# A written-out instruction order with a new price list: TensorE's changes of tile form counted one by one, paces and ranks set anew

## The chip, the cores and the metric

The kernel runs on one core of a Trainium2 chip. The metric is the device time of one execution in microseconds (us). Five engines work side by side, each through its own queue in a fixed order: TensorE (PE, with its weight loads shown apart as PEld), VectorE (DVE), ScalarE (ACT), GpSimd (POOL) and SyncE (SP). SP does no arithmetic here; it issues most of the DMAs. An instruction that waits holds up everything behind it in its own queue.

## The reference

Two stages follow each other. First comes attention with a hash mask, for 4 batches, 8 heads, 768 positions and head size 64:

```
q_bits = (q @ proj > 0); k_bits = (k @ proj > 0)        # 6 bits each
mask   = bucket(q_bits)[:, None] == bucket(k_bits)[None, :]
scores = where(mask, q @ k.T / 8, -1e9)
attn   = exp(scores - rowmax) / (sum + 1e-9)
x      = attn @ v                                        # heads joined: 768 x 512 a batch
```

Then comes a gated block for each batch, whose second matrix product mixes positions:

```
h = relu(x @ w_in)                       # 512 -> 1024, split into u and v
v_n = (v - mean) / sqrt(var + 1e-6)
v_s = w_spatial @ v_n + b_spatial        # 768 x 768 times 768 x 512
out = (u * v_s) @ w_out                  # 512 -> 512
```

## The kernel before

**Precision.** Operands of TensorE are float16, and each float32 operand is split into a high and a low half; a product is then three matmuls (high by high, high by low, low by high). Where an operand is turned to halves, ACT writes the high one and DVE or POOL subtracts it to get the low one. That is why "splits" and "rests" fill the vector engines.

**Attention.** Two heads make a pair; there are 16 pairs, four to a batch. A pair has six score steps, one for each block of 128 rows, so 96 steps in all; step S3.1 below is block 1 of pair 3 (pairs count from 0). A step (function `scores`, line 501) is 16 matmuls: three split products and one that adds the mask, which is made from the hash signs in the tile hk. They write two PSUM tiles sp, one for each head, and there is only one such pair of tiles to hand out, so **the next step cannot start before both heads' scores have been read**. For most heads (`by_queries`) DVE reads them with a running row maximum (ex<-sp, L525), ACT or POOL makes the bias (L532, L530), ACT takes the exponential (L535) and the high half (L539), DVE or POOL subtracts to get the low half (the "rest", pp<-ex,pp, L543), and SP issues a transposing DMA (pt<-pp, L547). A few steps later TensorE multiplies the result by v (pv, L653). Four heads, in pairs 1 to 4, go another way (`by_keys`): scores are computed turned, so no transpose is needed, but the row maxima must be known beforehand. For them TensorE computes half-price scores first (mx, `row_max`), DVE reduces them (L600), and at a pair's end a small vector of maxima is turned by TensorE (tp), copied by DVE (mt, L624) and sent by a DMA from SP into a row of the mask tile (hk<-mt, L627). The first score step of the next pair needs that DMA in its last four matmuls.

**The hash.** Before a pair begins, TensorE multiplies q and k by proj (hp, L371), DVE makes signs and scales them (sg, L378 and L382), and POOL issues eight or twelve small DMAs that put them into hk (hk<-sg, L393). The pair's q and k are split by ACT (L412) and DVE (hl, L416).

**The gated block.** As soon as a batch's four pairs are done, its work is queued in groups of matmuls (line 750): vps (x by the v half of w_in), ups (the u half), sps (the spatial product) and ops (the output). They fill TensorE between the score steps of the next batch. Before batch 0 is through, that is up to pair 4, no such filler exists. The last batch's block comes behind all scores. The weights come in 36 pieces; a piece is fetched by SP (raw or raws, L293), of which there are four places, and for the double-precision weights taken apart by DVE (w, L313 to L318) before it is halved (wi, ws, wo, L323 on ACT and L328 on DVE).

**What sets the order.** The kernel first lists every operation as an `Op`, with its engines, a length in the planner's own units, what it needs and a rank. The function `timetable` then plays a list scheduler over the five engines: whichever engine can start soonest takes the ready operation with the lowest key. Score steps have keys of their own and may not start before a pace (`begin`, which grows by one of the constants T_ from step to step). Where two engines can do an operation ("VG" for DVE or POOL, "AG" for ACT or POOL), the engine that comes free first takes it. LATE is an allowance added before a TensorE operation, other than a score step, that waits for another engine. W_EVERY spaces the weights' fetches in the plan. LATER shifts ranks by the operation's function name. Where the plan shows TensorE idle for over GAP it fills the hole with small matmuls that are thrown away (`warm`, L217). The operations are then written down in order of planned start. **Nothing of the plan's clock reaches the chip**: only the order on each engine, the choice of engine, and the number of warm matmuls do.

## Time and profile before

| | |
|---|---|
| median of 3 runs | 660.48 us (660.45 to 661.58) |
| the profiled execution's own time | 655.07 us |
| its span, first to last instruction | 653.3 us |
| PE busy | 615.5 us (94%) |
| DVE busy | 471.1 us (72%) |
| ACT busy | 473.7 us (73%) |
| POOL busy | 321.8 us (49%) |
| warm matmuls | 444 |
| rests (L543) on DVE and on POOL | 82 and 86 |

The profiled execution took 5.4 us less than the median of the runs, and 1.8 us of it lie outside the span. Busy time of an engine is the union of its instructions; a matmul's row is longer than the time to the next matmul, since they overlap. Views that group instructions give the count, the busy time, the mean length in ns, and then the idle time just before them with what ended it. A view by stages gives busy time of each engine in a stretch of the span.

### The profile page before, as it was taken

What the parts mean: (1) busy time and instruction counts of PE and PEld (TensorE: products, weight loads), DVE (VectorE), ACT (ScalarE), POOL (GpSimd) and SP (SyncE); (2) the same over time, 40 slices, a digit from 0 to 9 for tenths busy, and PEclk for the clock granted to TensorE, in tenths of its full rate; (3) what the DMA queues carried; (4) which work ended last, traced back from release to release, by engine and by line L of the source; (5) the groups of instructions that cost most, each with busy time, mean ns of one, the idle gap of its engine ahead of it and who ended that gap; (6) DMA issues with size and microseconds to landing.
All of it is one profiled execution on the core that took longest, in us unless ns stands there. A gap on an engine that the chain in (4) does not pass through costs nothing.

```text
span 653.3 us, 17683 instructions
## 1 busy us (share of the span) xinstructions
PE 615.5 (94%) x7076; PEld 374.4 (57%) x7076; DVE 471.1 (72%) x986; ACT 473.7 (73%) x800; POOL 321.8 (49%) x397
## 2 busy tenths in 40 slices
PE   5789999899999999899999999998999999999997
PEld 3466767577555656455555556564555665556553
DVE  6899999898788766758879677765667587365250
ACT  3868776868898977887879887876889967463121
POOL 4565451534686859494638559376749412000000
PEclk9999999999999999999999999999999999999999
DMA  5899988997899999999998999997997989210102
GB/s 186 197 190 227 199 163 174 222 214 145 178 209 188 169 219 198 204 209 198 212 207 147 201 225 148 227 213 138 210 214 130 153 150 158 50 49 0 49 1 96
DMA packets 311682, 108.94 MB, mean 167 GB/s; under 512 B 298144, under 2 KB 301744, under 8 KB 311600
## 3 DMA queue, kind: packets, MB, share of 16 engines
q1 hardware_dynamic: 306256, 106.26, 84.4%
q0 software_dynamic: 5248, 1.52, 1.2%
q8 instruction: 55, 0.90, 0.6%
q14 instruction: 27, 0.22, 0.1%
q10 hardware_dynamic: 96, 0.04, 0.0%
HBM read 27.94 MB, written 6.29 MB: 52 GB/s over the span
## 4 chain that ended last, share of the span: by engine, by line
PE 51%; DVE 15%; DMA 11%; ACT 9%; issue 7%; POOL 5%; SPq 1%; DVEq 0%; POOLq 0%; ACTq 0%
PE sps L750 12%; PE sp L496 9%; PE ops L750 9%; PE pv L653 8%; DMA pt<-pp 6%; PE ups L750 5%; DVE ex L525 4%; PE vps L750 3%; ACT pp L539 3%; ACT ex L535 2%; POOL pp L543 2%; DVE pp L543 2%; PE vpp L750 2%; DMA hk<-sg 2%; DVE mx L600 1%
## 5 line engine op out<-in xcount | busy, mean ns | idle before, releaser
L525 DVE TENSOR_SCALAR_CACHE_REDUCE ex<-sp 128x768 f32<-128x768 f32 x168 | 155.6, 951 | 55.1 <-PE sp L496 53.0
L543 POOL TENSOR_TENSOR pp<-ex,pp 128x768 f16<-128x768 f32 x86 | 140.9, 1646 | 74.2 <-ACT pp L539 53.0
L535 ACT ACTIVATE ex<-ex,nb 128x768 f32<-128x768 f32 x168 | 155.3, 932 | 10.5 <-POOL nb L530 7.3
L539 ACT CAST pp<-ex 128x768 f16<-128x768 f32 x168 | 137.3, 826 | 4.9 <-DMA pt<-pp 3.6
L653 PEld LDWEIGHTS <-pt 128*128 128x128 f16 x3024 | 107.4, 97 | 37.3 <-DMA pt<-pp 13.3
L653 PE MATMUL pv<-vp,pt 128*128 128x65 f16 x3024 | 118.6, 193 | 7.9 <-DMA pt<-pp 7.7
L496 PE MATMUL sp<-hl 64*128 64x384 f16 x1080 | 107.4, 324 | 5.0 <-DVE ex L525 4.7
L393 POOL DMA_DIRECT2D hk<-sg x156 | 79.8, 518 | 50.8 <-issue 15.9
L543 DVE TENSOR_TENSOR pp<-ex,pp 128x768 f16<-128x768 f32 x82 | 79.7, 980 | 34.2 <-ACT pp L539 33.9
L750 PE MATMUL sps<-ws,vn 128*128 128x384 f16 x576 | 100.8, 326 | 0.1
L496 PEld LDWEIGHTS <-hl 64*128 64x128 f16 x1116 | 51.1, 94 | 56.8 <-issue 27.5
L750 PEld LDWEIGHTS <-vn 128*128 128x128 f16 x576 | 53.7, 98 | 33.5 <-issue 0.9
L750 PE MATMUL ops<-wo,g 128*128 128x512 f16 x288 | 66.1, 379 | 1.0 <-DVE sg L378 1.0
L532 ACT ACTIVATE nb<-mr 128x1 f32<-128x1 f32 x123 | 24.1, 197 | 55.9 <-DVE ex L525 55.6
L750 PE MATMUL ups<-xt,wi 128*128 128x384 f16 x348 | 62.8, 326 | 1.2 <-ACT u L919 1.2
L750 PE MATMUL vps<-wi,xt 128*128 128x512 f16 x234 | 56.9, 379 | 1.7 <-DVE sg L378 0.9
L750 PEld LDWEIGHTS <-wi 128*128 128x128 f16 x384 | 35.1, 98 | 24.1 <-issue 3.7
L750 PEld LDWEIGHTS <-g 128*128 128x128 f16 x288 | 26.7, 98 | 31.7 <-issue 1.6
L750 PEld LDWEIGHTS <-xt 128*128 128x128 f16 x288 | 25.5, 97 | 29.5 <-issue 5.4
L496 PE MATMUL sp<-hk 12*128 12x384 f16 (+2 forms) x360 | 37.1, 329 | 4.5 <-DMA hk<-mt 3.5
L940 DVE SCALAR_TENSOR_TENSOR sy<-sps,bt 128x384 f32<-128x384 f32 x32 | 17.8, 555 | 31.0 <-PE sps L750 31.0
L948 ACT CAST g<-sy 128x384 f16<-128x384 f32 x32 | 16.2, 506 | 32.3 <-DVE sy L952 28.8
(112 smaller groups left out, 786.7 us busy)
## 6 DMA issues: line engine op xcount, KB each, us to landing
qk<-kq SPq DMA_DIRECT2D x16, 768.0 KB
out<-o SPq DMA_DIRECT2D x24, 256.0 KB
v<-v SPq DMA_DIRECT2D x12, 384.0 KB
pt<-pp SPq DMA_TRANSPOSE x168
hk<-sg POOLq DMA_DIRECT2D x156, 9.0 KB, 4.0
raw<-w_in SPq DMA_DIRECT2D x8, 256.0 KB
raws<-w_in SPq DMA_DIRECT2D x8, 256.0 KB
vf<-v SPq DMA_DIRECT2D x4, 384.0 KB
```

Of the source, the lines that this page charges most:

```text
L393: eng.dma_start(out=hkt(p)[D * e + at:D * e + at + 2 * NB, 1 - j // 2, (j % 2) * HS:(j % 2 + 1) * HS], in_=sg[1][32 * j + 16 * e:32 * j + ...
L496: nc.tensor.matmul(ps[e][:, c - halves[0]], lhsT=src[r, l, rows], rhs=src[r, m, cs], start=(a == 0), stop=(a == len(passes) - 1))
L525: nc.vector.tensor_scalar(ex, st["sc", p, i][e], -float(2 ** 28), None, op0=ALU.max, op1=ALU.max, accum_out=st["mx", n][:, i:i + 1])
L532: nc.scalar.activation(nb, mx, AF.Copy, scale=-ISQ)
L535: nc.scalar.activation(st["e32", n, i], st["e32", n, i], AF.Exp, bias=st["nb", n][:, i:i + 1], scale=ISQ)
L539: nc.scalar.copy(st["pp", n, i][:, 0], st["e32", n, i])
L543: eng.tensor_tensor(out=st["pp", n, i][:, 1], in0=st.pop(("e32", n, i)), in1=st["pp", n, i][:, 0], op=ALU.subtract)
L600: nc.vector.reduce_max(st["mx", 2 * p + e][:, i, c:c + 1], ps[e], axis=AX.XY)
L653: nc.tensor.matmul(o, lhsT=l, rhs=m, start=(i == 0 and k == 0), stop=(i == NT - 1 and k == len(todo_) - 1))
L750: nc.tensor.matmul(c[0], lhsT=l(), rhs=r(), start=(j == 0), stop=(j == len(products) - 1))
L940: nc.vector.scalar_tensor_tensor(out=y[0], in0=c[0], scalar=1.0 / (SN * SW), in1=bt[:, hs], op0=ALU.mult, op1=ALU.add)
L948: nc.scalar.copy(gt[h][0][:, d], y[0])
```

## The change

The planner now keeps the tile form that TensorE was last used in (128 rows, 64 for scores, 1 for the hash product) and adds FORM = 0.1 to an operation of another form. In exchange the lengths of the score step, the hash product and the pv product are set lower. The ranks (LATER), the pace, START, LATE and W_EVERY get new values. No operation of the kernel is added or removed.

```diff
+    FORM = 0.1
     X = 0.14
-    LATER = {'relu': 0.1, 'first': -0.5, 'bias': -0.3, 'bits': 0.1, 'stats': 0.3, 'half': -0.4, 'copy': 0.6, 'scale': 0.3, 'newton': -0.4, 'low': 0.6, 'exp': -0.1, 'factor': -0.3, 'turn': -0.6, 'rest': -0.1}
+    LATER = {'relu': -0.2, 'first': -0.8, 'bias': -0.4, 'bits': -0.5, 'stats': -0.3, 'half': -1.0, 'copy': 0.5, 'scale': 0.6, 'newton': -0.7, 'low': 0.6, 'exp': -0.1, 'factor': -0.4, 'turn': -0.6, 'rest': -0.1, 'move': -0.2, 'root': 0.3, 'lambda': 0.1}
...
+        form = [128]
...
             gap = t - free[e]
+            if e == "P" and o.form != form[0]:
+                form[0], o.d = o.form, o.d + FORM
...
-        t = op("P", 0.8, go, at["qk", p], *after, on=[qk], rank=(urgent(p), 3), need=("m", 1))
+        t = op("P", 0.65, go, at["qk", p], *after, on=[qk], rank=(urgent(p), 3), need=("m", 1), form=1)
...
-        t = op("P", 1.32 if four(p) else 1.42, go, *at["hl", p], *at["hk", p], on=[sc, held["hl", p], held["hk", p]], rank=(g, 0))
+        t = op("P", 1.21 if four(p) else 1.27, go, *at["hl", p], *at["hk", p], on=[sc, held["hl", p], held["hk", p]], rank=(g, 0), form=64)
...
-        at["pv", n] = op("P", 1.46 if n in WIDE else 0.57, go, at["pt", n, i], at["v", p] if n in WIDE else at["vp", p],
+        at["pv", n] = op("P", 1.46 if n in WIDE else 0.56, go, at["pt", n, i], at["v", p] if n in WIDE else at["vp", p],
...
-    T_FIRST, T_KEYS, T_QUERIES, T_THIRD, T_LAST = 5.0, 5.4, 5.55, 5.75, 5.95
-    START = 6.5
+    T_FIRST, T_KEYS, T_QUERIES, T_THIRD, T_LAST = 5.1, 5.2, 5.75, 5.55, 5.85
+    START = 8.5
...
-    LATE, LATE_D = 0.3, 2.25
+    LATE, LATE_D = 0.1, 2.25
...
-    W_FROM, W_EVERY = 21.0, 2.1
+    W_FROM, W_EVERY = 21.0, 1.6
```

The order of the whole program is new from the first warm matmuls on; three places show the kind of thing that moved. (Line numbers of the changed kernel are five higher.)

**First place: DVE at the turn from pair 2 to pair 3.** ex5_5 is the read of step S2.5, ex7_0 that of S3.0, ex7_1 that of S3.1; sg0_4, hl4 and sg1_4 are the hash signs and the split for pair 4; ws, wi and w are weights. Before, from the last rest of pair 2 on:

```order
L543 TENSOR_TENSOR pp5_5_1873<-ex5_5_1825,pp5_5_1873 128x768
L378 TENSOR_SCALAR sg0_4_1892<-hp4_1876,hc_73 128x384
L416 SCALAR_TENSOR_TENSOR hl4_1883<-qk4_1289,hl4_1883 128x768 x2
L382 TENSOR_SCALAR sg1_4_1969<-sg0_4_1892,hc_73 128x384
L328 SCALAR_TENSOR_TENSOR ws1_80<-raw16_1818,ws0_79 128x384
L328 SCALAR_TENSOR_TENSOR ws1_80<-raw17_1827,ws0_79 128x384
L328 SCALAR_TENSOR_TENSOR wi1_102<-w15_1823,wi0_101 128x256
L328 SCALAR_TENSOR_TENSOR ws1_80<-raws_299,ws0_79 128x384
L525 TENSOR_SCALAR ex7_0_1986,mr7_1984<-sp3_0_1_1853 128x768
```

Now:

```order
L548 TENSOR_TENSOR pp5_5_1840<-ex5_5_1808,pp5_5_1840 128x768
L323 SCALAR_TENSOR_TENSOR w14_1801<-raws_294,w14_1801 128x256
L333 SCALAR_TENSOR_TENSOR wi1_102<-w13_1716,wi0_101 128x256
L530 TENSOR_SCALAR ex7_0_1897,mr7_1895<-sp3_0_1_1864 128x768
L383 TENSOR_SCALAR sg0_4_1919<-hp4_1887,hc_73 128x384
L421 SCALAR_TENSOR_TENSOR hl4_1893<-qk4_1317,hl4_1893 128x768 x2
L387 TENSOR_SCALAR sg1_4_1951<-sg0_4_1919,hc_73 128x384
L318 TENSOR_SCALAR w15_1947<-w15_1947 128x256
L530 TENSOR_SCALAR ex7_1_1975,mr7_1895<-sp3_1_1_1929 128x768
```

Four weight pieces, the hash signs and the split stood between the rest and the read of S3.0; now two other weight pieces do, and the signs and the split stand behind that read.

**Second place: SP's queue at the end of pair 3.** mt8 is the vector of maxima that step S4.0 needs, pt7_4 the transpose of step S3.4. Before:

```order
L293 DMA raws_299<-w_out 128x256
L547 DMA_TRANSPOSE pt7_4_2349<-pp7_4_2305 128x12x128
L627 DMA hk1_82<-mt8_2347 1x6x128
L547 DMA_TRANSPOSE pt7_5_2455<-pp7_5_2446 128x12x128
L293 DMA raws_299<-w_out 128x256
```

Now:

```order
L552 DMA_TRANSPOSE pt7_4_2306<-pp7_4_2245 128x12x128
L298 DMA raws_294<-w_sp 128x384
L298 DMA raw25_2349<-w_sp 128x384
L298 DMA raws_294<-w_sp 128x384
L632 DMA hk1_82<-mt8_2364 1x6x128
L552 DMA_TRANSPOSE pt7_5_2402<-pp7_5_2371 128x12x128
```

The transpose that was directly ahead of mt8 now has three weight fetches between it and mt8.

**Third place: DVE inside pair 5**, between the two reads of step S5.3 (ex10_3 and ex11_3). Before, two rows stood between them:

```order
L525 TENSOR_SCALAR ex10_3_3202,mr10_2955<-sp5_3_0_3167 128x768
L839 BN_STATS bs0_1_3210<-vr0_1_3200 128x6
L840 BN_AGGR mv0_0_3090<-bs0_1_3210 128x2
L525 TENSOR_SCALAR ex11_3_3253,mr11_2962<-sp5_3_1_3168 128x768
```

Now nine:

```order
L530 TENSOR_SCALAR ex10_3_3220,mr10_2912<-sp5_3_0_3129 128x768
L866 TENSOR_SCALAR ve0_0_3227<-mv0_0_2896 128x3
L421 SCALAR_TENSOR_TENSOR hl6_2909<-qk6_2760,hl6_2909 128x768
L876 TENSOR_TENSOR ve0_0_3227<-ve0_0_3227,rs0_0_3249 128x3
L877 SCALAR_TENSOR_TENSOR ve0_0_3227<-ve0_0_3227,rs0_0_3249 128x3
L878 SCALAR_TENSOR_TENSOR rs0_0_3249<-ve0_0_3227,rs0_0_3249 128x3
L879 SCALAR_TENSOR_TENSOR ve0_0_3227<-mv0_0_2896,rs0_0_3249 128x3
L421 SCALAR_TENSOR_TENSOR hl6_2909<-qk6_2760,hl6_2909 128x768
L844 BN_STATS bs0_4_3290<-vr0_4_3264 128x6
L845 BN_AGGR mv0_3_3210<-bs0_4_3290 128x2
L530 TENSOR_SCALAR ex11_3_3300,mr11_2940<-sp5_3_1_3130 128x768
```

The normalization of batch 0 and both splits for pair 6 have moved between the two reads. Counted over the program, DVE has 91 rests now and POOL 77 (82 and 86 before); the warm matmuls are 361 (444 before); TensorE's order changes its form 221 times (223 before).

## The prediction

> **What bounds the kernel now.** I read the page first, then the busy time by stages cut at pair borders, then the waits and timelines of the two longest score steps. From the page, the span and its engines:

> ```profile
> span 653.3 us, 17683 instructions
> PE 615.5 (94%) x7076; PEld 374.4 (57%) x7076; DVE 471.1 (72%) x986; ACT 473.7 (73%) x800; POOL 321.8 (49%) x397
> ```

> TensorE is idle for 653.3 - 615.5 = 37.8 us. Its busy time also holds the 444 warm matmuls that stand in its order, which compute nothing. The timeline of TensorE over the two longest steps gives the price of one, and prices I need later:

> ```profile
> 107.56 0.50 PE L496 MATMUL sp<-hk 64*128 64x384 f16 x4 [1.36 <-DMA hk<-mt]
> 107.99 0.85 PE L371 MATMUL hp<-qk,hc 128*32 128x384 f32 x8
> ...
> 110.71 2.73 PE L217 MATMUL warm<-ident 128*128 128x128 f16 x46
> 113.28 0.71 PE L653 MATMUL pv<-vp,pt 128*128 128x65 f16 x18
> 113.92 0.33 PE L496 MATMUL sp<-hl 64*128 64x384 f16 x1
> ...
> 137.28 1.53 PE L653 MATMUL pv<-vf,ex 128*128 128x65 f32 x12
> 138.65 3.12 PE L217 MATMUL warm<-ident 128*128 128x128 f16 x53
> 141.70 1.15 PE L496 MATMUL sp<-hl 64*128 64x384 f16 x12
> 144.13 0.50 PE L496 MATMUL sp<-hk 64*128 64x384 f16 x4 [1.28 <-DMA hk<-mt]
> ```

> 46 warm matmuls fill 110.71 to 113.28, so 0.056 us each, and 444 of them 24.9 us. What TensorE does not spend on the kernel is thus 37.8 + 24.9 = 62.7 us; the rest is work that no order changes. The question is where those 62.7 us lie. By stages (us, then busy time of PE, PEld, DVE, ACT, POOL, the granted clock, DMA), cut where pairs 0 to 7 begin, then one late row:

> ```profile
> 13.20:47.20 34.00, 26.59 (x386) 17.47 (x385) 27.23 (x64) 23.16 (x40) 21.43 (x27) 1.00 0.92 183
> 47.20:77.00 29.80, 27.82 (x334) 19.94 (x335) 28.62 (x71) 23.84 (x44) 13.27 (x16) 1.00 1.00 207
> 77.00:104.50 27.50, 25.80 (x313) 18.71 (x312) 26.89 (x69) 19.81 (x38) 12.48 (x16) 1.00 0.91 183
> 104.50:141.70 37.20, 33.81 (x423) 25.60 (x421) 33.81 (x74) 27.02 (x50) 14.77 (x18) 1.00 0.95 209
> 141.70:168.60 26.90, 24.95 (x310) 17.93 (x308) 24.23 (x60) 20.24 (x37) 13.10 (x22) 1.00 0.81 186
> 168.60:200.60 32.00, 30.39 (x362) 16.54 (x363) 26.50 (x56) 28.22 (x49) 25.13 (x28) 1.00 1.00 174
> 200.60:235.20 34.60, 33.31 (x425) 19.90 (x424) 24.06 (x48) 32.43 (x57) 24.34 (x31) 1.00 1.10 183
> 235.20:270.00 34.80, 32.21 (x442) 19.62 (x441) 25.11 (x50) 27.16 (x44) 23.27 (x26) 1.00 1.11 202
> 270.00:412.00 142.00, 140.64 (x1733) 81.22 (x1734) 106.51 (x202) 117.59 (x193) 89.31 (x109) 1.00 1.07 195
> ```

> From 13.2 to 168.6 us (pairs 0 to 4) TensorE is idle for 16.4 us and spends about 255 warm matmuls, 14.3 us: half of all that is lost lies here. And here DVE is the full engine: 113.6 us busy of 121.4 in pairs 1 to 4. From 270 to 412 TensorE loses 1.4 of 142 us: there it is the bound itself, and an order can gain next to nothing.

> The mechanism shows in the step from 104.5 to 113.92, which takes 9.4 us where a usual one takes 4 to 6. This is DVE in the same stretch:

> ```profile
> 109.45 1.82 DVE L416 SCALAR_TENSOR_TENSOR hl<-qk,hl 128x768 f16<-128x768 f32 x2
> ...
> 113.15 0.95 DVE L525 TENSOR_SCALAR_CACHE_REDUCE ex<-sp 128x768 f32<-128x768 f32 x1
> ```

> S3.0 was computed at 108.06, but its read began only at 113.15, behind signs, split and four weight pieces; S3.1 could not start before it. At the pair's other end S4.0 hung on the vector of maxima. From DVE, SP's queue and the chain of waits there:

> ```profile
> 135.69 0.20 DVE L624 COPY mt<-tp 6x128 f16<-6x128 f16 x1
> 136.21 2.57 SPq L547 DMA_TRANSPOSE pt<-pp  x1
> 138.88 5.21 DMA hk<-mt
> ```

> The copy was there at 135.89, its DMA left at 138.88, behind a transpose.

> **The change part by part.** Only order, choice of engine and warm matmuls can reach the chip. The form count itself is nearly void: 221 changes for 223. A change costs about 0.1 us: in these rows of a late stretch, 15 matmuls and the change to the score step take 2.53 us, and 15 times 0.1625 (the 144 that follow each other at the end) are 2.44.

> ```profile
> 382.18 2.60 PE L750 MATMUL sps<-ws,vn 128*128 128x384 f16 x15
> 384.71 1.15 PE L496 MATMUL sp<-hl 64*128 64x384 f16 x12
> ...
> 610.13 23.56 PE L750 MATMUL sps<-ws,vn 128*128 128x384 f16 x144
> 633.53 15.70 PE L750 MATMUL ops<-wo,g 128*128 128x512 f16 x72
> ```

> So two fewer: -0.2 us (between -0.2 and 0).

> *Pairs 0 to 4.* I counted in both orders what DVE has before the first matmul of S5.0. It loses 11 instructions that take weights apart (2 of L313, 3 each of L314, L316, L318) and 3 weight halves (L328), and gains 2 rests. Their rows (L316, of the same kind as L318, at the latter's price):

> ```profile
> L313 DVE TENSOR_SCALAR w<-w 128x256 f32<-128x256 f32 x24 | 8.6, 363 | 1.5 <-ACT w L309 1.5
> L314 DVE TENSOR_SCALAR w<-w 128x256 uint32<-128x256 uint32 x24 | 7.3, 309 | 0.0
> L318 DVE SCALAR_TENSOR_TENSOR w<-raws,w 128x256 uint32<-128x256 uint32 x12 | 5.6, 465 | 0.0
> L328 DVE SCALAR_TENSOR_TENSOR ws<-raws,ws 128x384 f16<-128x384 f32 x6 | 3.3, 548 | 0.0
> L543 DVE TENSOR_TENSOR pp<-ex,pp 128x768 f16<-128x768 f32 x82 | 79.7, 980 | 34.2 <-ACT pp L539 33.9
> ```

> -(2 x 0.363 + 3 x 0.309 + 6 x 0.465 + 3 x 0.548) + 2 x 0.98 = -6.1 + 2.0 = -4.1 us of DVE. DVE is busy for 140.8 of the 155.4 us of this stage, 0.91, so I take 0.91 x 4.1 = **-3.7 us**. Two things that I looked at agree in sign: 62 warm matmuls fewer are written there (193 for 255; 62 x 0.056 = 3.5), and the two orders shown: the read of S3.0 no longer waits for the split (up to 113.15 - 108.06 = 5.1 us earlier, of which the later row-max work, ordered behind the same hash, gives some back), and mt8 follows three short issues in place of a transpose (up to 138.88 - 135.89 = 3.0 us). Bounds: 0 if the hash and maxima chain holds the pairs at their old pace, -6 if the two long steps shrink as shown.

> In that shorter stage TensorE also does more: 6 more vps matmuls and 6 more wide pv products stand ahead of S5.0. Their prices: a wide pv product is two rows of pv<-vf, so 12 rows in 137.28 to 138.65 make 6 products, 1.37 us. For vps:

> ```profile
> 475.18 1.94 PE vps L750 x9
> ```

> 1.94 / 9 = 0.216, six are 1.3. Together 2.7 us of work leave the later part, where TensorE is the bound: **-2.7 us** (0 to -2.7).

> *Pairs 5 to 7.* The weights and rests that left come here. DVE has 13 us more than before between S5.0 and S8.0 (8 rests of 0.98, 14 weight pieces, some of the block's own), on 75.7 busy of 101.4: 88 us, 87%. ACT has 1.6 us more on 87.8. 16 more warm matmuls are planned (41 for 25), +0.9. For stalls: in the row 304.6 to 339.5 below, DVE at 84% left TensorE no idle time; the far bound is that every one of the 10 rests that DVE has more up to S8.0 delays a score read in full, 10 x 0.98 = 9.8. I take **+2.9** in all, 0.9 and 2.0, close to the near row, since filler is there.

> ```profile
> 304.60:339.50 34.90, 34.90 (x408) 18.49 (x407) 29.15 (x58) 28.33 (x48) 15.80 (x21) 1.00 1.14 216
> ```

> *S8.0 to the end.* 42 warm matmuls for 82: -2.2 at most. Against it, LATE is 0.2 smaller: TensorE's products are placed that much closer behind their producers. What such waits cost before is the idle time ahead of these groups:

> ```profile
> L750 PE MATMUL ops<-wo,g 128*128 128x512 f16 x288 | 66.1, 379 | 1.0 <-DVE sg L378 1.0
> L750 PE MATMUL ups<-xt,wi 128*128 128x384 f16 x348 | 62.8, 326 | 1.2 <-ACT u L919 1.2
> L750 PE MATMUL vps<-wi,xt 128*128 128x512 f16 x234 | 56.9, 379 | 1.7 <-DVE sg L378 0.9 <-ACT vr L833 0.7
> ```

> 3.9 us; taken as waits of about 0.6 us (an estimate, as 0.7, 0.9 and 1.0 stand in these rows), some seven places, and 0.2 more in each is +1.4. Between -2.2 and +1.4 I take the middle, **-0.4**.

> *Start and pair 0.* 85 and 96 warm matmuls for 82 and 92: 7 x 0.056 = **+0.4**; what lies ahead of the first step is written as before but for those.

> Sum: -0.2 - 3.7 - 2.7 + 2.9 - 0.4 + 0.4 = **-3.7 us**, on a span of 653.3 us whose execution took 655.07. The median of the runs is 660.48, 5.4 above that execution; I carry the difference over unchanged: **656.8 us**.

> **The rivals.**

> *A larger gain.* The planned holes go and nothing takes their place: -4.1, -2.7, +0.9, -2.2, +0.4, -0.2 give -7.9: 652.6. For it speaks that 83 fewer warm matmuls stand in the program; against it, that pairs 5 to 7 get DVE and ACT near full.

> *No change.* The maxima's chain (hash DMA, row maxima, turned vector, DMA) holds pairs 1 to 4 at their old pace, so the -3.7 falls away: 660.5 within measurement. The two hk<-mt waits of 1.36 and 1.28 us speak for it; the five and three us in which nothing but a queue's order held the chain speak against.

> *Slower: reads of scores behind rests in pairs 5 to 7.* There is one pair of score tiles, so a read that DVE makes late stops TensorE at the next step. Without the 2.0 the sum is -5.7; if all 10 rests fall on the path, +9.8 leaves +4.1: 664.6. It decides from about six of the ten. For it speaks the third place of the order, seven more DVE rows between the two reads of S5.3; against it, 24 vps matmuls stand behind S5.3 in the new order (24 x 0.216 = 5.2 us), which cover the four to five us of those rows.

> *Slower: TensorE's clock.* Where warm matmuls go, a wait is left as idle time. Ahead of S4.0 53 of them, 3.12 us, are gone, and 1.28 us of waiting already stand there. The granted clock is 1.00 in every stage above, and 5.43 us of idle time at the start are followed by a slow hash product:

> ```profile
> 5.43 1.50 PE L371 MATMUL hp<-qk,hc 128*32 128x384 f32 x8 [5.43 <-DMA qk<-kq]
> ```

> 1.50 us where the later one at 107.99 took 0.85. [...]

> That the change does nothing is excluded: nearly every row moves.

> **How the numbers follow.** What a measurement can tell from no change is about 0.2%, 1.3 us. Forecast, -1.4 to -6 us: 0.43. Larger gain: 0.16. No change: 0.15. Slower by the reads: 0.20, by the clock: 0.06. Faster 0.59, same 0.15, slower 0.26. The likeliest case's own range is 654.4 to 659.1; to hold 8 in 10 it must take in most of the larger gain and the smaller outcomes of the slower cases: 652.0 to 663.0.

> **What would show it.** Right: S3.0 to S3.1 well under 9.4 us and S4.0's last matmuls before 142; S5.0 starts 2 to 5 us before 168.6; TensorE's idle time in pairs 5 to 7 grows by less than 3 us over 5.5; the last score step starts 5 to 8 us before 548, since more work stands behind it (9 more vpp matmuls at 0.216 and 6 more sps at 0.1625, 2.9 us). Wrong: DVE as full as before with S5.0 no earlier (the chain bounds), or sp<-ex waits of several us between 165 and 270 (the reads), or a granted clock under 1.00 before 145.

## The result, and the profile after

| | before | after |
|---|---|---|
| median of 15 runs each, us | 659.12 (655.01 to 661.58) | 664.46 (659.97 to 671.2) |
| ratio after to before | | 1.0084, 95% interval 1.0058 to 1.0109 |
| profiled execution, us | 655.07 | 667.3 |
| its span, us | 653.3 | 665.5 |
| mean granted clock in it | 1.000 | 0.985 |
| TensorE idle in it, us | 37.8 | 43.5 |

The change makes the kernel 0.8% slower; 656.8 was forecast. Here and below a median is over all executions, and a ratio with its interval compares only those within 1.5% of the fastest of the same kernel, so that the quotient of two medians can differ from it. First the page of the kernel after, its span and the busy time of the engines:

```profile
span 665.5 us, 17515 instructions
PE 622.0 (93%) x6993; PEld 376.6 (57%) x6993; DVE 475.5 (71%) x994; ACT 475.4 (71%) x807; POOL 309.3 (46%) x382
```

TensorE runs 83 matmuls fewer (all of them warm ones) and is busy for 6.5 us more. The same work has become longer, and the view by stages says where. These are the stages of the prediction, cut where pairs 0 to 7 now begin, and then the late row; the columns are the stretch, its length, busy time of PE, PEld, DVE, ACT and POOL, the granted clock and the DMAs' share and GB/s:

```profile
14.80:48.00 33.20, 28.60 (x391) 18.70 (x389) 27.73 (x66) 22.95 (x40) 19.58 (x26) 0.95 0.95 182
48.00:82.50 34.50, 29.45 (x339) 20.48 (x338) 28.77 (x73) 24.11 (x44) 14.05 (x18) 0.95 0.99 181
82.50:116.10 33.60, 29.18 (x322) 21.01 (x323) 28.86 (x70) 22.16 (x41) 10.63 (x12) 0.90 0.70 151
116.10:146.40 30.30, 29.59 (x358) 21.43 (x359) 29.17 (x65) 23.52 (x42) 15.76 (x20) 1.00 1.11 227
146.40:174.30 27.90, 26.52 (x314) 19.38 (x313) 26.59 (x61) 23.34 (x41) 12.09 (x18) 1.00 0.93 191
174.30:209.30 35.00, 33.75 (x366) 17.66 (x365) 29.39 (x70) 28.38 (x52) 16.61 (x22) 0.95 0.93 175
209.30:247.40 38.10, 36.58 (x458) 22.22 (x459) 27.47 (x52) 33.84 (x58) 25.12 (x30) 1.00 1.06 184
247.40:279.80 32.40, 29.15 (x416) 18.20 (x415) 26.67 (x49) 25.80 (x42) 18.42 (x24) 1.00 1.08 192
279.80:416.10 136.30, 131.10 (x1651) 76.08 (x1648) 103.53 (x206) 114.43 (x190) 81.27 (x99) 1.00 1.11 201
```

Read it against the rows of before. Pair 3 went from 37.2 to 30.3 us. Pairs 1 and 2 went the other way, from 29.8 to 34.5 and from 27.5 to 33.6, and in them the clock, 1.00 everywhere before, is 0.95 and 0.90. DVE, which was the full engine there (28.62 of 29.80 and 26.89 of 27.50), now stands idle for 5.7 and 4.7 us. TensorE's idle time grew by 3.1 and 2.7 us in these two pairs, and by as much it fell in pairs 0 and 3: over pairs 0 to 4 it is 16.2 us for 16.4, and what is longer there is the busy time, 143.3 for 139.0. The two new holes show in TensorE's timeline (start, length, line, tiles, how many, and in brackets the idle time just before with what ended it):

```profile
51.34 0.33 PE L501 MATMUL mx<-hl 64*128 64x384 f16 x1
54.87 0.32 PE L501 MATMUL mx<-hk 63*128 63x384 f16 x1 [3.19 <-DMA hk<-sg]
...
56.95 2.36 PE L501 MATMUL sp<-ws 64*128 64x384 f16 x16
...
62.16 1.46 PE L501 MATMUL sp<-ws 64*128 64x384 f16 x15 [0.61 <-DVE ex L530]
...
82.45 1.15 PE L501 MATMUL sp<-hl 64*128 64x384 f16 x12
86.92 0.82 PE L501 MATMUL sp<-hk 64*128 64x384 f16 x4 [3.31 <-DMA hk<-mt]
87.67 1.16 PE L658 MATMUL pv<-vp,pt 128*128 128x65 f16 x18
88.64 1.90 PE L222 MATMUL warm<-ident 128*128 128x128 f16 x16
90.47 0.50 PE L501 MATMUL mx<-hl 64*128 64x384 f16 x1
```

After 3.19 us of waiting, 16 score matmuls take 2.36 us; 15 of the same kind a step later take 1.46. After 3.31 us of waiting, 16 warm ones fill 88.64 to 90.47, which is 0.114 each where the kernel before paid 0.056. So each hole is paid for twice: once as idle time, and once more by slow work behind it. The clock itself, in stretches of 3.41 us laid so that they fit the places where it changes (columns as above; 0.50 in the eighth is half speed):

```profile
51.99:55.40 3.41, 0.48 (x2) 0.19 (x2) 1.07 (x4) 3.16 (x6) 1.64 (x1) 1.00 0.80 133
55.40:58.82 3.42, 3.41 (x31) 1.90 (x32) 2.48 (x5) 0.00 (x0) 0.00 (x0) 0.50 1.25 262
82.71:86.12 3.41, 0.89 (x12) 0.40 (x9) 2.89 (x10) 1.61 (x3) 1.19 (x3) 1.00 0.95 327
86.12:89.53 3.41, 2.61 (x31) 1.99 (x31) 1.60 (x4) 1.68 (x4) 0.00 (x0) 0.50 1.04 185
89.53:92.94 3.41, 3.41 (x25) 1.90 (x23) 1.66 (x4) 1.62 (x3) 1.64 (x1) 0.50 0.15 45
174.87:178.29 3.42, 2.17 (x20) 0.65 (x16) 2.18 (x6) 1.59 (x2) 0.52 (x1) 1.00 1.24 237
178.29:181.70 3.41, 3.41 (x31) 1.73 (x24) 2.93 (x8) 2.96 (x6) 0.93 (x2) 0.50 0.87 165
290.92:294.33 3.41, 1.95 (x25) 0.81 (x24) 2.47 (x5) 2.86 (x7) 3.39 (x4) 1.00 0.87 161
294.33:297.74 3.41, 3.41 (x51) 2.28 (x47) 0.29 (x2) 3.31 (x6) 3.24 (x4) 1.00 1.02 272
```

There are five such places before the last product: 24.7, 55.4, 86.1 (6.8 us), 178.3 and 420.6, together 20.5 us at half clock, which can cost up to 10.2 us. The profiles differ by 12.2. Idle time is 5.7 us more (5.1 of it behind the start of S8.0), and 83 warm matmuls fewer are 4.6 less: 10.2 + 5.7 - 4.6 = 11.3 of 12.2. The medians are only 5.3 apart: the profile of before is of one of its shortest executions, at full clock.

Where does the first hole come from? In the old order one of the two first row maxima of pair 2 stood ahead of S1.1 and one behind it; in the new order both stand ahead. And the hash rows that they need came late. From the DMA groups between 40 and 56 us, of the kernel before and then after (KB each, median us from issue to landing):

```profile
hk<-sg POOLq DMA_DIRECT2D x8, 9.0 KB, 3.2
```

```profile
hk<-sg POOLq DMA_DIRECT2D x8, 9.0 KB, 7.9
```

The eight small transfers were the same. What changed is what ran beside them (tested below, in c_load). Before, POOL issued them from 43.07 on and SP sent 768 KB of q and k for pair 3 at 46.65; after, they left from 44.58 on, and the large load at 45.18. The second hole is the vector of maxima mt4: in the new order the hash of pair 3 stands at the end of S1.4, right ahead of the turning of mt4, and DVE does signs, two splits, a rest, the scaling and pieces of weights before it copies the vector at 80.19, 4.7 us after it was turned at 75.5. The rest of the wait is the vector's DMA: SP issues it at 80.86, right behind another 768 KB of q and k (79.90), and the four products that need it start at 86.92. Before, the same load and the same DMA followed each other at 73.27 and 74.25, and the products, wanted at 78.1, started at 78.95.

### The profile page after: what moved, and what is told of

Same layout as the page of the kernel before. It is cut to its first block, busy times and chain, and to the rows that moved or that the text cites. A ratio compares the mean times of both kernels' runs of the same rounds, so it can differ in the third digit from the quotient of the medians.

```text
span 665.5 us, 17515 instructions
## 1 busy us (share of the span) xinstructions
PE 622.0 (93%) x6993; PEld 376.6 (57%) x6993; DVE 475.5 (71%) x994; ACT 475.4 (71%) x807; POOL 309.3 (46%) x382
## 5 line engine op out<-in xcount | busy, mean ns | idle before, releaser
L548 POOL TENSOR_TENSOR pp<-ex,pp 128x768 f16<-128x768 f32 x77 | 126.4, 1648 | 87.9 <-ACT pp L544 78.4
L658 PEld LDWEIGHTS <-pt 128*128 128x128 f16 x3024 | 109.2, 98 | 47.5 <-DMA pt<-pp 23.6
L658 PE MATMUL pv<-vp,pt 128*128 128x65 f16 x3024 | 120.4, 194 | 15.3 <-DMA pt<-pp 14.7
L548 DVE TENSOR_TENSOR pp<-ex,pp 128x768 f16<-128x768 f32 x91 | 86.5, 963 | 39.3 <-ACT pp L544 39.0
L501 PE MATMUL sp<-hl 64*128 64x384 f16 x1080 | 109.6, 327 | 3.3 <-DVE ex L530 3.2
L501 PE MATMUL sp<-hk 12*128 12x384 f16 (+2 forms) x360 | 39.8, 334 | 4.9 <-DMA hk<-mt 3.3
```

Of the source, the lines that this page charges most:

```text
L501: nc.tensor.matmul(ps[e][:, c - halves[0]], lhsT=src[r, l, rows], rhs=src[r, m, cs], start=(a == 0), stop=(a == len(passes) - 1))
L548: eng.tensor_tensor(out=st["pp", n, i][:, 1], in0=st.pop(("e32", n, i)), in1=st["pp", n, i][:, 0], op=ALU.subtract)
L658: nc.tensor.matmul(o, lhsT=l, rhs=m, start=(i == 0 and k == 0), stop=(i == NT - 1 and k == len(todo_) - 1))
```

## The experiments

Two theories stood against each other. **Clock**: the time is lost because TensorE's clock falls to half behind holes that the plan no longer fills. **Waits**: it is lost to the waits themselves, and the clock is a small matter. Half-clock time below is (1 - mean clock) x time / 0.5, taken from the clock of each run.

### Take the warm matmuls out of the kernel before (b_nowarm)

```
-        for t, n in fill:
+        for t, n in fill[:2]:
```

> The kernel before, without the 362 warm matmuls behind the first score step (the 82 ahead of it stay); what the program computes and its order are otherwise unchanged. Theory CLOCK (the loss of the changed kernel is TensorE at half clock in stretches of 3.4 us behind holes in its work): the holes that the warm matmuls filled now leave TensorE idle, the granted clock falls below 1.00 in four to ten stretches, and each costs up to 1.7 us: 5 to 15 us slower than before, mean clock 0.97 to 0.99. Rival WAITS (the loss is the new waits themselves, the clock costs nothing that matters): 362 x 0.056 = 20 us of filler fewer, most of it inside waits that stay; no slower than before, up to 5 us faster.

Measured: 666.86, ratio 1.0076 (1.0038 to 1.0115), median clock 0.968. TensorE has 362 matmuls, some 20 us, less to do and the kernel gets slower. Two stretches that follow each other in its trace:

```profile
44.59:48.00 3.41, 1.10 (x30) 0.99 (x31) 3.41 (x13) 1.53 (x5) 3.21 (x6) 1.00 0.73 161
48.00:51.41 3.41, 2.69 (x25) 1.34 (x22) 3.41 (x8) 3.23 (x6) 1.53 (x4) 0.50 0.86 172
```

The waits theory is refuted as the whole account: the order was left alone, and by that theory the kernel could not get slower. The clock fell a little further than the 0.97 to 0.99 expected.

### Fill the five holes of the kernel after (a_fill)

```
+        for g, j, n in ((1, 0, 20), (6, 2, 45), (72, 2, 28)):      # step, place in it, matmuls
+            op("P", 0.07 * n, lambda n=n: warm(n)).start = line[at_ + j].start - 1e-6
+    MID = {(2, 0): 45, (5, 0): 20}          # inside S2.0 and S5.0, ahead of the products with hk
```

> The changed kernel with 158 more warm matmuls, order otherwise the same, at the five places ahead of which its trace shows the waits that came before a half-clock stretch: 20 ahead of step S0.1, 45 ahead of the first mx of pair 2 (a wait of 3.19 us), 45 inside S2.0 ahead of its last four matmuls (3.31 us), 20 inside S5.0 (1.24 us), 28 ahead of a pv in S12.0 (1.88 us). CLOCK: the waits stay as long but the clock stays at 1.00 in most runs, mean 0.997 or more; 5 to 8 us faster than the changed kernel's 664.5, so 656 to 660 and about 0.995 to 1.00 of before. WAITS: the same time as the changed kernel, 1.008 of before, or up to 3 us more where the filler outlasts the wait.

Measured: 658.88 (before beside it 659.36), ratio to before 0.9996 (0.9965 to 1.0028), median clock 0.993. That is 5.6 us below the kernel after: 158 matmuls that compute nothing take back the whole loss, though only to a tie. The gain that was forecast is not there: with the clock at 0.997 its profile still spends 64.1 us in pairs 1 and 2, where the kernel before spends 57.3, and that eats the 6.9 us of pair 3. This part is not the clock's; that it is the waits' is tested in c_load and c_all.

The runs themselves price the clock. Over the runs of the kernel before in the three sets of experiments, time rises with half-clock time by 0.41 to 0.47 us for each us (correlation 0.76 to 0.87). Over the 15 runs of the kernel after it is 0.43, with a correlation of only 0.55. The kernel before has 6.6 us of it in its median run, the kernel after 16.0. At 0.4 that is 3.8 of the 5.3 us between them. With a full clock they would, by this estimate, stand at about 656.5 and 658.1. The price does not cover all that the fills brought: the median went from 16.0 to 9.2 us at half clock, 2.7 us at 0.4, and the time fell by 5.6. An interval reaches some 2 us to either side; whether the rest is more than that stays open.

### Move the two late pieces back (a_order)

```
+        late = step(7)                              # S1.1
+        for k, o in enumerate(MAXIMA[2, 0]):        # first row maxima of pair 2: behind it
+            o.start = late.start + 1e-6 * (k + 1)
...
+        copied.start = turned.start + turned.d + 0.1     # DVE's copy of mt4: right behind its turning
+        moved.start = copied.start + copied.d            # and its DMA
```

> The changed kernel with two things put back where the kernel before has them, no warm matmul added: the first two mx products of pair 2 stand behind step S1.1 in place of ahead of it (so TensorE does not stop for the hash DMA), and DVE's copy of the maxima vector mt4 with its DMA stands ahead of the split for pair 3 and of the transpose (so S2.0 does not stop 3.3 us). CLOCK: two waits of 3.2 and 3.3 us and the three half-clock stretches behind them (5.1 us) go: mean clock 0.993 or more, 6 to 9 us faster than the changed kernel, 0.995 to 1.00 of before. WAITS: the waits alone go: 3 to 6 us faster, and it does not matter what the clock shows.

Measured: 669.03, ratio 1.0091 (1.0052 to 1.0129). Both theories missed. Of its seven executions four took 663.6 to 669.0, as the kernel after, and three 675.5 to 676.3; the only trace is of one of those three, so what it shows need not hold for the four. Its TensorE timeline shows what took the places:

```profile
58.60 1.16 PE L673 MATMUL pv<-vp,pt 128*128 128x65 f16 x18 [4.14 <-DMA pt<-pp]
...
100.65 0.32 PE L515 MATMUL mx<-hk 63*128 63x384 f16 x1 [2.17 <-DMA hk<-sg]
```

The wait for hk had covered one for a transposed block, which SP issued at 49.0, right behind the same 768 KB at 48.6; the wait for mt4 had covered the hash rows of pair 3, whose scaling still came late on DVE, at 91.6. In this execution one hole is larger than the one it replaced (4.14 for 3.19) and the other smaller (2.17 for 3.31), and 3.4 us at half clock follow from 58.0 and 17.1 from 68.3. Which wait is named in a profile is only the last of several.

### Undo one number (u_late)

```
-    LATE, LATE_D = 0.1, 2.25
+    LATE, LATE_D = 0.3, 2.25
```

> The changed kernel with LATE back at 0.3 from 0.1, planned anew: 621 warm matmuls for 361, the hash product of pair 3 back in S1.2 (S1.4 in the changed kernel) and 71 rests on DVE for 91. If LATE is the part of the change that places work so close that holes open: the waits over 2 us between 48 and 90 us go, the clock is 0.995 or more, and the time is 655 to 660. If not: 662 or more, with holes elsewhere.

Measured: 696.16, ratio 1.0533 (1.047 to 1.0597): 32 us slower than the kernel after, with 132.3 us behind the last score step in place of 109.2. The theory that LATE alone opens the holes is refuted. The other expectation, 662 or more with holes elsewhere, holds (a wait of 4.20 us for another vector of maxima stands ahead of 54.9), but by how much it would be slower was not foreseen. This number of the planner is no part that can be taken out; with another value it writes another program.

### The same fills at a quarter of the work (a_fill32)

By then a rule could be read off the six traces there were (before, after, b_nowarm, a_fill, a_order, u_late). Lay a grid of 3.41 us over each. Count for each stretch what its matmuls use of the array: rows x columns in use x streamed columns, against 128 x 128 x all cycles at full clock (a float32 matmul counted twice). A stretch under 0.38 was followed by one at half clock, a stretch over it by one at full clock, with 6 exceptions in 1,155 stretches, all between 0.37 and 0.39. In the traces of before and after alone, six stretches stand ahead of half clock and count 0.05 to 0.35; all others count 0.386 or more. In the view by stretches above, the one from 174.87 is busy for 2.17 us, but half of that with products of 12 rows and with hash products on 32 columns: 0.27, and half clock follows. The one from 290.92 is busy for less, 1.95, but uses 0.42: full clock follows. Columns count as rows do: with 128 columns for every product, the stretches ahead of three of the five falls of the kernel after (24.7, 178.3, 420.6) would stand at 0.54 to 0.91. To test the rows:

```
...
-            nc.tensor.matmul(b[:, :P], lhsT=ident, rhs=ident, start=True, stop=True)
+            nc.tensor.matmul(b[:, :P], lhsT=ident[:k], rhs=ident[:k], start=True, stop=True)   # k = 32 for the fills
```

> The changed kernel with the same 158 filling matmuls at the same five places as in the run called a_fill, but each on 32 of the 128 rows: as long in TensorE's time, a quarter of its work. Work theory (the granted clock of a stretch of 3.41 us follows from the stretch before: half where its matmuls use less than about 0.38 of the array's rows x columns x cycles; read off the traces so far): counted on a_fill's trace with the fills at a quarter, the places where such a stretch can begin add up to 12 us against 7, so the mean clock falls by about 0.004 against a_fill and the time comes out near 661 (5.4 us x 0.42 = 2.3 above a_fill's 658.9), with half-clock stretches again near 53 to 56 or 84 to 87 us. Busy theory (it follows from how long TensorE stands idle, whatever it multiplies): as a_fill, 658.9, clock 0.993.

Measured: 661.55 beside 660.74 for before, ratio 1.0007 (0.9976 to 1.0038); clock 0.9915. In time the two theories are too close to be told apart (a_fill's interval overlaps). The trace tells them apart. At the hole of S1.0, shifted to 57 us here, in the timeline, in the groups by form (the timeline names only the form of the first, one of five planned ones) and by stretches:

```profile
56.40 3.07 PE L226 MATMUL warm<-ident 128*128 128x128 f16 x50
```

```profile
L226 PE MATMUL warm<-ident 32*128 32x128 f16 x45 | 2.7, 214 | 0.0
```

```profile
57.05:60.46 3.41, 3.17 (x47) 2.54 (x45) 1.44 (x5) 3.27 (x6) 1.64 (x1) 1.00 0.95 210
60.46:63.87 3.41, 3.34 (x31) 1.88 (x32) 2.41 (x5) 0.00 (x0) 0.00 (x0) 0.50 1.25 238
```

TensorE was busy for 3.17 of 3.41 us, and the clock fell all the same: 45 of those matmuls used a quarter of the rows, and the stretch counts 0.23. In a_fill, with 128 rows, the stretch behind this hole kept its clock. Over the eight kernels that ran after the 0.38 was written down, the rule has no exception in 1,543 stretches, 33 of them ahead of half clock; by busy time alone the best threshold misplaces 18. The limit is sharp only as far as a matmul's columns can be placed in time: laid differently over its row in the trace, up to five of these stretches miss it, at 0.34 to 0.41.

### Fill the holes of the kernel before (b_fill)

```
+    MID = {(0, 0): 12, (3, 0): 22}
+        for g, j, n in ((1, 0, 18), (1, 3, 14), (2, 3, 16), (20, 1, 26), (47, 3, 24)):
```

> The kernel before with 130 filling matmuls of 128 rows ahead of its own seven waits in pairs 0, 3 and 7 (products of the first score step, the row maxima of the first three steps, score step 3.0 and 3.2, the weighted sum of step 7.5). Work theory: the kernel before loses about 6.6 us at half clock in its median run (clock 0.995), each worth 0.41 us by the line through its 24 runs; with the fills the clock is 0.998 or more and the median 656.5 to 657.5, 1.7 to 2.7 below before. Theory that only the waits count: no gain, 0 to 1.5 slower by what the fills overhang the waits, 659 to 661.

Measured: 662.58 beside 660.74, ratio 1.0027 (0.9995 to 1.0059); clock 0.997. The clock did what the work theory says, and the time did not follow; it came out above both expectations. Two of the fills:

```profile
24.25 0.94 PE L221 MATMUL warm<-ident 128*128 128x128 f16 x14 [0.65 <-DVE mx L614]
...
28.57 1.05 PE L221 MATMUL warm<-ident 128*128 128x128 f16 x16 [0.87 <-DVE mx L614]
```

They take a PSUM bank of the same pool as the row maxima behind them, so they wait for the same reduction and run after the wait, not in it. The others may delay what stands behind them wherever the wait of that run is shorter; that was not traced. By this account a fill is free only while the wait that it covers is there.

### Load later, and all waits together (c_load, c_all)

c_load is a_fill with the large load behind the first transpose of S0.5, and 15 fills for 45 at S1.0:

```
...
+        qk_ = at["qk", 3]
+        behind = [o for o in turn_ if o.start > qk_.start][1]
+        qk_.start = behind.start + 1e-3
```

> a_fill with one load put later: the 768 KB of q and k for pair 3, on SP's queue, from ahead of the transposes of step 0.4 to behind the first transpose of step 0.5, about 6 us; and 15 in place of 45 filling matmuls ahead of the row maxima of step 1.0. Queueing theory (the hash rows of pair 2 landed 6 us after their issue because this load was ahead of them; before they took about 3): they land about 3 us earlier, step 1.1 begins 2 to 3 us earlier and the whole comes out near 656.5 to 657. Rival: another transfer or DVE work is as late there: 658 to 660 as a_fill.

Measured: 664.41, ratio 1.0074 (1.0042 to 1.0107). The mechanism is right at its place. From its DMA groups between 43 and 60 us:

```profile
hk<-sg POOLq DMA_DIRECT2D x8, 9.0 KB, 4.7
```

The hash rows land in 4.7 us for 7.9, the wait for them is gone, and S1.1 begins 5.5 us after S1.0 (8.5 in a_fill). The pair as a whole gets only 0.5 us shorter: a row maximum (0.73 us) and a score read (0.76) are waited for next, and with 30 fills fewer 3.41 us at half clock begin at 58.7, which a_fill does not have. And the kernel loses more elsewhere than it gains: pair 6 takes 44.8 us for 38.2, with a score read 2.94 us late and 6.8 us of half clock. Why that read comes late there was not settled.

c_all adds to it:

```
+        go_.start = step(9).start - 1e-4               # hash products of pair 3 ahead of S1.3
+        bits_.start = step(9).start + 1.4              # their signs on DVE
+        scale_.start = bits_.start + 0.01              # and scaling
...
+        for k, o in enumerate(moves_[:8]):
+            o.start = none_.start - 0.02 + 1e-4 * k    # their DMAs on POOL
...
+        copied.start = turned.start + turned.d + 0.1   # mt4's copy, as in a_order
```

> c_load, and in addition the hash products of pair 3 ahead of step 1.3 (where the kernel before nearly has them, there in step 1.2) with their two DVE operations and their eight DMAs moved up with them, DVE's copy of the turned maxima of pair 2 right behind their transposition, 15 in place of 45 fills in step 2.0, and 58 fills more in steps 0.0, 0.1, 0.2 and 4.2. Waits theory: the two waits of 3.2 and 3.3 us are gone without others in their place, pairs 1 and 2 last about 59 us together in place of 64 (a_fill) and 57 (before), and the time is 653 to 655, below both kernels. Rival (the plan has no slack there: DVE's work at the boundary of pairs 1 and 2 or the transposes by DMA set the end, and what one wait gives up the next takes): 657 to 660.

Measured: 658.56 beside 660.74, ratio 0.9978 (0.9946 to 1.0011); clock 0.9955. Pairs 1 and 2 by stages, to be read against 34.50 and 33.60 above:

```profile
50.40:82.50 32.10, 28.79 (x353) 20.69 (x353) 29.16 (x69) 22.87 (x42) 15.47 (x18) 1.00 0.89 184
82.50:111.50 29.00, 27.38 (x337) 20.23 (x338) 28.74 (x71) 22.31 (x41) 9.03 (x9) 1.00 0.78 171
```

Together 61.1 us, where 59 was expected: 7.0 less than the kernel after, still 3.8 more than before. Of the 10.8 us that the two pairs had lost, 4.0 came back with the fills alone (64.1 in a_fill) and 3.0 with the pieces and the load moved; the waits for hk are gone from both. The other 3.8 stay open; 30 fills (1.7 us) stand in these pairs that the kernel before doesn't have, perhaps some of them on the path. Pairs 0 to 4 together take 155.8 us in this trace, 155.4 before: with the holes closed and the clock full the stage is as long as it was, and not shorter. The time falls in the rival's range, and that it is below the kernel before is not shown: the interval reaches 1.0011.

### A last fit of the fills (c_best)

```
-        for g, j, n in ((1, 0, 20), (1, 3, 10), (2, 3, 18), (6, 2, 15), (26, 2, 10), (72, 2, 28)):
+        for g, j, n in ((1, 0, 20), (6, 2, 15), (8, 0, 10), (8, 3, 8), (8, 4, 14), (26, 2, 10), (72, 2, 28), (76, 7, 30)):
```

> c_all without its 28 fills ahead of the second and third row maxima of step 0.1 and 0.2 (in c_all's trace these ran 0.65 and 1.19 us after the wait that they were to cover, since they need the same PSUM bank), and with 62 more where a stretch can still fall below 0.38: ahead of step 1.2's scores 10, behind its row maxima 8 and 14, and ahead of the last weighted sum of step 12.4, which waited 2.2 us, 30. Work theory with the waits as in c_all: 1.6 us of fills off the path and the median run's 5.9 us at half clock down to 2 to 3, times 0.45: 655 to 656.5, 0.5 to 0.8 per cent below before. Rival (the fills or the new phases of the waits cost what they save): 658 to 660.

Measured: 659.38 beside 659.56, ratio 0.9967 (0.9929 to 1.0005); clock 0.9935. The medians differ by 0.2 us, and the interval reaches beyond 1: the time lies in the rival's range, and that it beats before is again not shown. The 655 to 656.5 were missed, and the clock that was to bring them did not rise.

### Each part alone (d_form, d_ranks, d_pace)

Into the kernel before go only the counted forms with the three new lengths; only the new LATER; only the new T_ and START:

```
+            if e == "P" and o.form != form[0]:
+                form[0], o.d = o.form, o.d + FORM
...
-    T_FIRST, T_KEYS, T_QUERIES, T_THIRD, T_LAST = 5.0, 5.4, 5.55, 5.75, 5.95
-    START = 6.5
+    T_FIRST, T_KEYS, T_QUERIES, T_THIRD, T_LAST = 5.1, 5.2, 5.75, 5.55, 5.85
+    START = 8.5
```

> The kernel before with the counted changes of form alone (its own ranks, pace, start and allowance): the plan puts 567 warm matmuls in place of 444. Theory that the parts add: this and the next two differ from before by amounts whose sum is near the whole change's +5. Theory that each new number makes another plan whose waits fall anew: each lies somewhere within 15 us of before, and the sum says nothing; its time is then read from its own holes and clock.

> The kernel before with the new table of ranks alone. Parts add: see d_form. If the new ranks alone put the sign bits' scaling late on DVE and so the hash rows late, waits for hk of 2 us and more stand in pairs 1 and 2 as in the whole change, and it is slower than before by 3 to 8; if the pace did it, they don't.

> The kernel before with the new steps per pair and the later start alone. Parts add: see d_form. If the pace put the large load ahead of the hash rows, waits for hk of 2 us and more stand in pair 1, and it is slower than before by 3 to 8; if the ranks did it, they don't.

| | median, us | ratio to before, interval | us behind the last score step |
|---|---|---|---|
| before (beside them) | 659.56 | | 105.3 |
| forms alone | 693.67 | 1.0504 (1.0443 to 1.0564) | 132.5 |
| ranks alone | 692.28 | 1.0474 (1.0401 to 1.0547) | 122.4 |
| pace alone | 677.98 | 1.029 (1.0231 to 1.0349) | 120.0 |
| all (after) | 664.46 | 1.0084 (1.0058 to 1.0109) | 109.2 |

Their losses add up to 85 us; the whole change costs 5.3. The theory that the parts add is refuted. The other one was right that the sum says nothing, but its 15 us were missed by all three, by 3 to 19 us. Each has 15 to 27 us more behind the last score step; why was not settled. Nor is the wait for the hash rows pinned on a part: the longest wait for hk in the traces is 1.90 us with the ranks alone and 1.32 with the pace alone, under the 2 us expected of whichever made it. Pairs 1 and 2 together take 71.5 us with the forms alone and 67.6 with the ranks alone, as much as in the whole change (68.0), and 58.5 with the pace alone, near the 57.3 of before. So far as these runs go, the numbers fit only together; LATE and W_EVERY were not put into the kernel before alone.

## Why the prediction was wrong

**The sum's base.** It was made on an execution with a clock of 1.000. Half-clock time was already costing the kernel before about 2.6 us in its median run (6.6 x 0.4), and no term of the sum held what the change does to it.

**Pairs 0 to 4 (-3.7) and the work carried (-2.7): the step that failed.** The stage measured +4.1 in the profiles (155.4 to 159.5): -0.8, +4.7, +6.1, -6.9 and +1.0 for its five pairs. What I showed of the order came true. S3.1 now follows S3.0 after 3.4 us, where it was 9.4:

```profile
116.06 1.15 PE L501 MATMUL sp<-hl 64*128 64x384 f16 x12
...
118.25 1.24 PE L222 MATMUL warm<-ident 128*128 128x128 f16 x19
119.42 1.15 PE L501 MATMUL sp<-hl 64*128 64x384 f16 x12
```

Pair 3 gained 6.9 us by it. But S5.0 starts at 174.3, 5.7 later than 168.6, where 2 to 5 earlier was forecast. The step took DVE's work for the limit of the whole stage and checked the order at its two longest steps only. In pairs 1 and 2 the new order made the hash rows and the maxima late, and less DVE work could gain nothing there. Nor did DVE's work shrink: it is busy for 141.1 us of the stage, 140.8 before, where 4.1 less was counted. With S5.0 late, four of the 14 weight pieces counted out of the stage were done within it after all. And the clock took its share: four of the six half-clock stretches lie in this stage, at 0.4 some 5.5 us. A full clock alone does not bring the forecast back, as the 155.8 us of c_all show. The 6 vps matmuls and 6 wide products did move ahead of S5.0, but what lies behind it grew by 6.5 us in place of shrinking by their 2.7. The vector that counted was mt4; I had looked at mt6 and mt8. The bound of 0 for the case that "the hash and maxima chain holds the pairs at their old pace" was itself too kind: a new order can make that chain slower.

**The rival of the clock** named the right loss, slow work of TensorE behind a hole, gave it a chance of 0.06, and looked for the hole where warm matmuls go, ahead of S4.0. The holes opened where waits grew and no filler had been planned, and at five places. The trace of before, with a clock of 1.00 in every stage, has no fall of the clock to price; in that of after one lasts 3.41 us, once 6.83, and 3.41 us cost about 1.4 at the estimate of 0.4.

**Pairs 5 to 7 (+2.9)** measured +4.1 (101.4 to 105.5), one half-clock stretch of about 1.4 within it; the idle time there grew from 5.5 to 6.0 us, as forecast. But 15 matmuls of ops, 3.2 us at 0.216, had moved into this stage from behind it, which no term held, so that the agreement in size is in part luck. The rival of late score reads is refuted: TensorE waits for none in this stage (0.8 us before).

**S8.0 to the end (-0.4)** measured +2.4 (383.3 to 385.7), again with one half-clock stretch. The smaller LATE was priced on the wrong products: the 3.9 us of waits ahead of ops, ups and vps are 0.0 in the page of after, and the waits that grew are those of pv for a transposed block. PE's groups from S8.0 on, before and after (the columns are count, busy time, mean ns of one, idle time just before):

```profile
L653 PE MATMUL pv<-vp,pt 128*128 128x65 f16 (+1 forms) x1800 | 70.6, 193 | 2.1 <-DMA pt<-pp 2.1
L658 PE MATMUL pv<-vp,pt 128*128 128x65 f16 (+1 forms) x1803 | 71.8, 194 | 10.4 <-DMA pt<-pp 10.3
```

The growth of 8.2 us is more than that of all idle time (5.7); that LATE made it is not shown. In a_fill, c_all and c_best they are still 7.3, 6.8 and 5.8 us, and no run was made to close them; b_fill, in the old order, has 5.4, so part of it may be the execution and not the order. What it is worth stays open. Behind the last score step, 2.9 us more work was foreseen and 3.9 us came. **Start and pair 0 (+0.4)** measured +0.9. **The forms (-0.2)** cannot be seen in any run. The price of a change holds: in the trace of before 0.258 us pass from a matmul of 128 rows and 384 columns to a score matmul, and 0.162 from one of the former to the next.

The sign that I had named for a wrong prediction was the one that came: a granted clock under 1.00 before 145.

## What to carry to other kernels

When an order is rewritten, list every wait of the old trace and check in the new order what each producer now stands behind, at all places and not only at those that the change improves; a shorter hole at one place says nothing about the next. Price a hole on TensorE as its length plus the slow work behind it (here 3.19 us of waiting and then 3.41 us at half clock), and look at the granted clock by stages before any wait. Four parts of this change, put in or taken out one at a time, made programs 18 to 34 us slower; numbers of a planner that were chosen together are better not judged one by one: rerun the whole choice, with the clock in its price list.

## What the runs showed of the hardware

The grid does not start with the kernel: counted from the first instruction, its first line lies at 0.2 us in b_nowarm, 0.8 in after, 1.5 in before, 2.4 in a_fill32 and 3.4 in a_order. That offers an account of why equal runs differ, the same holes falling into one stretch or being split over two. It is argued and not shown, since each kernel has one trace; what the runs show is that the kernel before had a mean clock between 0.984 and 1.000 and times from 655 to 666 us, with the two going together (correlation 0.76 to 0.87).
